# Seven products of a group in one PSUM bank, the second added by TensorE on a copy of the first

## The chip, the cores and the metric

The kernel runs on one core of a Trainium2 chip. The metric is the device time of one execution in microseconds (us), as the median of several runs. The engines of the core work side by side, each through its own list of instructions in a fixed order: TensorE (PE, matrix products into the accumulator memory PSUM), VectorE (DVE), ScalarE (ACT), GpSimd (POOL) and SyncE (SP, which starts transfers). An instruction that needs another engine's result waits on a semaphore, and everything behind it on its engine waits with it. PSUM has eight banks here, each of 128 partitions by 512 float32 columns.

## The reference

Two branches read the normalised input and are multiplied; shapes are 2048 rows by 512, the hidden layer has 1376 columns, and there are 32 heads of 16.

```python
def _A_ref(x, wqkv, wo):
    ...
    phi = lambda t: jnp.where(t > 0, t + 1, jnp.exp(t)) + 1e-6
    pq, pk = phi(q), phi(k)
    kv = jnp.einsum("bhsd,bhse->bhde", pk, v)
    z = jnp.einsum("bhsd->bhd", pk)
    num = jnp.einsum("bhqd,bhde->bhqe", pq, kv)
    den = jnp.einsum("bhqd,bhd->bhq", pq, z)[..., None] + 1e-6
    ...
    return o @ wo

def _B_ref(x, w1, w2, w3, w4):
    h = _gelu(_layernorm(x, axis=-1) @ w1)
    ...
    hs = jnp.concatenate([g0, g1, g2, g3], axis=-1) @ w2
    x1 = x + hs
    h2 = _gelu(_layernorm(x1, axis=-1) @ w3) @ w4
    return x1 + h2

xn = _layernorm(x, axis=-1)
return x + _A_ref(xn, wqkv, wo) * _silu(_B_ref(xn, w1, w2, w3, w4))
```

g0 to g3 are quarters of the columns of h, shifted by +1, -1, +2 and -2 rows.

## The kernel before, in words

The 2048 rows are worked in four quarters of 512. Every product of float32 matrices is split: each operand is a high part plus a low part (names that end in h and l), and `products` (L514) issues three matmuls for each term: high by high, high by low, low by high. All of them stand under L151 in the profile, copies and activations of ACT under L173, sums of two operands on DVE under L198.

Many of the larger products are formed by blocks in seven products instead of eight. `seven` (L948) does this for results 256 columns wide (TH = 256); it is called for 36 groups: 8 by `mix2` (L1047, the product with w2), 12 by `up_plain` and 8 by `up_pair` (L1270 and L1293, the product with w3 and its GELU), 8 by `attend_pair` (L1463). `keys_queries` (L914) does the same 512 wide, six times. Each product of a group has two terms, so six matmuls. A group takes three PSUM banks of the pool `mm`, of which `seven` uses half each: pa, pb and pe. Its steps are: product a11 b11 into pb; ACT copies pb to p1 in SBUF; product a12 b21 into pa; DVE adds pa and p1 to the first result, z[0]; s1 t1 into pe; ACT copies pe to p5; s2 t2 is accumulated on pb, and ACT copies that to u2; s4 b22 is accumulated on pe, and DVE adds u2 and pe; s3 t3 on pb, and DVE adds pb and p5; a22 t4 on pb, which is the last result. In the profile the names have m, s or k behind them for `mix2`, `attend_pair` and `keys_queries`, and none for the products with w3, where the first result is called gf.

The order of the instructions is worked out ahead by a planner (class `Plan`, L89). `add` (L99) records each operation with what it reads and writes as spans of columns of a tile; an operation depends on an earlier one where their spans of one tile overlap. With `behind` (L146) a matmul can be recorded as writing more than it does, a whole tile for example. `emit` (L296) then lists the operations by their costs and due times, engine by engine, and the code is issued in that order. A table of numbers, `SOONER` (L1746, some 170 pairs), moves the due times of single operations. The planner also hands out PSUM banks: four in the pool `acc`, four in `mm` (L475).

The semaphores are set when the planned order is issued: for each tile, an instruction that touches it waits for those issued before it on other engines that touch the same tile, if one of the two writes.

Of the kernel before, what the change touches and what calls it, by code (L numbers as in the profile page):

```python
# [9 lines left out]
F32 = mybir.dt.float32  # L10
# [5 lines left out]
P = 128  # L16
# [414 lines left out]
def linear_attn_gated_by_mixer(  # L431
# [40 lines left out]
    RB = 32  # L472

    space = bass.MemoryType.PSUM
    counts = {"w": 2, "p": 98, "h": 6, "sm": 10, "acc": 4, "mm": 4}  # L475
    const = ctx.enter_context(tc.tile_pool(name="const", bufs=1))
    pools = {}
    for tag, n in counts.items():
        kw = {"space": space} if tag in ("acc", "mm") else {}
        pools[tag] = ctx.enter_context(tc.tile_pool(name=tag, bufs=1, **kw))  # L480
    pools["dram"] = ctx.enter_context(tc.tile_pool(name="dram", bufs=1, space=bass.MemoryType.DRAM))
    pl = Plan(nc, pools, counts, ("acc", "mm"))

    def piece(name, dt=F32):
        return pl.new("p", name, dt, PIECE)[:, :512]
# [8 lines left out]
    def bank(name):  # L494
        return pl.new("mm", name, F32, 512)[:, :]
# [18 lines left out]
    def products(ps, terms, start=True, stop=True, more=False, behind=None):  # L514

        ms = []
        for sh, sl, mh, ml in terms:
            ms += [(sh, mh), (sh, ml), (sl, mh)]
        for n, (s, m) in enumerate(ms):
            pl.mm(ps, s, m, start and n == 0, stop and n == len(ms) - 1, more=more, behind=None if n else behind)  # L520
# [374 lines left out]
                TW[f"t{n + 1}"].append(hl)  # L895
        TW["b11"], TW["b21"], TW["b22"] = WK.hl[:2], WK.hl[2:], WQ.hl[2:]

    def seven_in_two(go, pb, pe, p5, first, z1, z2):

        go(pb, "a11", "b11", True)  # L900
        go(pe, "s1", "t1", True)
        pl.act(p5, pe, AF.Copy)
        pl.act(pe, pb, AF.Copy)
        go(pe, "a12", "b21", False)
        go(pb, "s2", "t2", False)
        first(pe)
        pl.act(pe, pb, AF.Copy)
        go(pb, "s3", "t3", False)
        go(pe, "s4", "b22", False)
        pl.tt(z2, pb, p5, ALU.add)  # L910
        pl.tt(z1, pe, p5, ALU.add)
        go(pb, "a22", "t4", False)

    def keys_queries(b, j):  # L914

        i, k = b * QT + j, b * QT + j + 2
        pa, pb, pe = (bank(f"{n}k{i}") for n in ("pa", "pb", "pe"))
        p1, p5, u2 = (piece(f"{n}k{i}") for n in ("p1", "p5", "u2"))

        def go(ps, x, y, start=True):  # L920
            products(ps, [both(U[b][x][c], j * P, (j + 1) * P) + TW[y][c] for c in range(2)], start, more=not start)

        go(pb, "a11", "b11")
        pl.act(p1, pb, AF.Copy)
        go(pe, "s1", "t1")
        pl.act(p5, pe, AF.Copy)
        go(pb, "s2", "t2", False)
        pl.act(u2, pb, AF.Copy)
        go(pa, "a12", "b21")
        pl.tt(p1, pa, p1, ALU.add)  # L930
        go(pb, "s3", "t3", False)
        pl.tt(p5, pb, p5, ALU.add)
        go(pe, "s4", "b22", False)
        pl.tt(u2, u2, pe, ALU.add)
        feature_k(i, p1, True)
        go(pb, "a22", "t4", False)
        feature_k(k, pb, True)
        feature_q(i, u2)
        feature_q(k, p5)
# [5 lines left out]

    def seven(name, z, prod):  # L948

        pa, pb, pe = (bank(f"{n}{name}").cols(0, TH) for n in ("pa", "pb", "pe"))  # L950
        p1, p5, u2 = (pl.new("h", f"{n}{name}", F32, TH).all for n in ("p1", "p5", "u2"))

        def go(ps, x, y, start=True):
            products(ps, prod(x, y), start, more=not start)

        go(pb, "a11", "b11")
        pl.act(p1, pb, AF.Copy)
        go(pa, "a12", "b21")
        pl.tt(z[0], pa, p1, ALU.add)
        go(pe, "s1", "t1")  # L960
        pl.act(p5, pe, AF.Copy)
        go(pb, "s2", "t2", False)
        pl.act(u2, pb, AF.Copy)
        go(pe, "s4", "b22", False)
        pl.tt(z[1], u2, pe, ALU.add)
        go(pb, "s3", "t3", False)
        pl.tt(z[2], pb, p5, ALU.add)
        go(pb, "a22", "t4", False)
        return pb

    def right(views, place):
# [75 lines left out]
    def mix2(i):  # L1047

        b, j = divmod(i, QT)
        o1, o2 = piece(f"o{i}"), piece(f"o{i + 2}")  # L1050

        def prod(x, y):
            return [both(AH[b][x], c * TH + j * P, c * TH + (j + 1) * P) + BW[y][c] for c in range(2)]

        ps = seven(f"m{i}", [o1.cols(0, TH), o1.cols(TH, 512), o2.cols(TH, 512)], prod)
        pl.act(o2.cols(0, TH), ps, AF.Copy)
        for k, o in ((i, o1), (i + 2, o2)):
            pl.gather(o, X[k])
            mixed(k, o)
# [210 lines left out]
    def up_plain(b, s):  # L1270
        hi, lo = zip(*(rounds(f"f{b}_{f}") for f in (s, s + NS)))
        c1, c2 = (piece(f"gf{b}_{f}") for f in (s, s + NS))
        z = c1.cols(0, TH), c1.cols(TH, 512), c2.cols(TH, 512)
        ps = seven(f"{b}_{s}", z, lambda x, y: [AF3[s][x][c] + YT[b][y][c] for c in range(2)])
        pl.act(hi[0], c1, AF.Gelu_apprx_tanh)
        pl.act(c1, c1, AF.Gelu_apprx_tanh)
        split(lo[0], c1, hi[0])
        pl.act(hi[1].cols(TH, 512), z[2], AF.Gelu_apprx_tanh)
        pl.act(z[2], z[2], AF.Gelu_apprx_tanh)
        pl.act(hi[1].cols(0, TH), ps, AF.Gelu_apprx_tanh)  # L1280
        pl.act(c2.cols(0, TH), ps, AF.Gelu_apprx_tanh)
        split(lo[1], c2, hi[1])
        for k, f in enumerate((s, s + NS)):
            H3[b, f] = (hi[k], lo[k], P)
# [8 lines left out]
    def up_pair(b, s):  # L1293
# [6 lines left out]
        s14, s23 = piece(f"sf{b}_{s}a"), piece(f"sf{b}_{s}b")  # L1300
        n1, n4 = s14.cols(0, TH), s14.cols(TH, 512)
        n2, n3 = s23.cols(0, TH), s23.cols(TH, 512)
        ps = seven(f"{b}_{s}", z, lambda x, y: [AF3[s][x][c] + YT[b][y][c] for c in range(2)])
        f = F4[b, s] = {}

        first = len(pl.ops)

        def keep(name, v, src):
            t = piece(f"f{b}_{s}{name}", F32R)
# [2 lines left out]
            pl.act(v, src, AF.Gelu_apprx_tanh)  # L1312
            split(f[name][1], v, f[name][0])

        pl.act(z[1], z[1], AF.Gelu_apprx_tanh)
        keep("a11", z[0], z[0])
        pl.tt(n3, z[0], z[1], ALU.subtract)
        keep("a22", z[2], z[2])
        pl.tt(n1, z[1], z[2], ALU.add)
# [6 lines left out]
        hl = rounds(f"f{b}_{s}s")  # L1326
        rounded(*hl, s14)
        f["s1"], f["s4"] = both(hl, 0, TH), both(hl, TH, 512)
        for op in pl.ops[first:]:
            op.patience = HURRY  # L1330
            pl.soon(op)

    STREAM = ("a1", "a11", "b11"), ("a4", "a22", "t4"), ("a2", "a12", "b21"), ("a5", "s1", "t1"), ("a3", "s4", "b22")
    CHAIN = None, ("s2", "t2"), ("s3", "t3")
# [128 lines left out]
    def attend_pair(i):  # L1463
        b, k = divmod(i, QT)
        k //= 2
        o1, o2 = SO[b, k, 0], SO[b, k, 1] = piece(f"so{i}"), piece(f"so{i + 1}")
        z = [o1.cols(0, TH), o1.cols(TH, 512), o2.cols(TH, 512), o2.cols(0, TH)]
# [28 lines left out]

    warm = bank("warm")
    for n in range(WARM):  # L1500
        pl.mm(warm.cols(n % NC * P, (n % NC + 1) * P), ones.all, ones.all, True, True, slow=True)
# [21 lines left out]
    scale_x(0, 1)  # L1523
    scale_x(1, 1)
    scale_x(2, 2)
    ks = [bank(f"k{i}") for i in range(QT)]
    ksum = pl.new("acc", "ksum", F32, 512).all
    for i in range(2):
        raw_k(ks[i], i)
# [136 lines left out]
    for b in range(NQ):  # L1666
# [77 lines left out]
                gate(b, QT - 1, r, a, TH, xr=xr[QT - 1], whole=a > 0)  # L1744

    SOONER = (  # L1746
# [16 lines left out]
    )  # L1763
    pl.emit(first=6.0, lead={"p": 14.0, "w": 14.0}, reserve={"p": 20, "w": 1}, window=12.0,
            ahead=6.0, table=SOONER)
# [37 lines left out]
```

## Time and profile before

| | us |
|---|---|
| median of 3 runs | 502.05 (502.02 to 502.64) |
| span of the profiled execution | 501.2 |
| PE busy | 494.3 |
| DVE busy | 440.9 |
| ACT busy | 388.9 |
| POOL busy | 84.9 |

The profiled execution has a span of 501.2 us from the first to the last instruction; its own time outside the profiler isn't listed apart, and the median is 0.85 above the span. Busy times are sums over an engine's instructions. In rows that list a group of instructions the columns are: line, engine, operation, the tile written and those read, size, count, then busy us and mean ns of one, then us of idle time ahead of them on that engine and what ended most of it. In a timeline a row is start us, duration us, engine, line, operation. A row of the waits reads: who waited for whom, us in total, times, longest. A row of the windows reads: stretch, its length, then busy us and count of PE, PEld (TensorE's loading of weights), DVE, ACT, POOL, then TensorE's granted clock, the share of the transfer engines and GB/s.

### The profile page before, as it was taken

How to read it: one execution, taken by the hardware profiler on the slowest of the kernel's cores; microseconds unless marked ns; L12 is line 12 of the kernel's file. 1: busy time of each engine (PE TensorE's matmuls, PEld its weight loads, DVE VectorE, ACT ScalarE, POOL GpSimd, SP SyncE). 2: the span in 40 equal slices, each digit the busy share in tenths (PEclk: the TensorE clock that was granted, in tenths of full speed). 3: DMA queues.
4: the chain of work that ended last, by engine and by line, in shares of the span. 5: the costliest groups of instructions: out<-in, count | busy, mean ns of one | idle time of the engine just before them, and what ended most of it. 6: DMA issues, size and time to landing. Idle time of an engine off the chain costs nothing.

```text
span 501.2 us, 9464 instructions
## 1 busy us (share of the span) xinstructions
PE 494.3 (99%) x3102; PEld 442.2 (88%) x3102; DVE 440.9 (88%) x944; ACT 388.9 (78%) x859; POOL 84.9 (17%) x97
## 2 busy tenths in 40 slices
PE   8999999999999999999999999999999999999996
PEld 6777887898888888899999989999899998999986
DVE  5989999999699995999999998897799969998364
ACT  5999899867798884977777579957699878977551
POOL 1344433131221122020100002200020200201100
PEclk9999999999999999999999999999999999999999
DMA  7949985479994799979897599978699887898604
GB/s 245 365 110 239 319 261 144 106 149 269 322 260 134 191 336 233 262 198 286 266 319 243 193 312 260 269 235 245 190 252 305 225 192 239 278 314 266 154 8 120
DMA packets 86989, 116.69 MB, mean 233 GB/s; under 512 B 8864, under 2 KB 41148, under 8 KB 86940
## 3 DMA queue, kind: packets, MB, share of 16 engines
q1 hardware_dynamic: 77004, 98.00, 60.3%
q0 software_dynamic: 9936, 18.09, 20.9%
q8 instruction: 24, 0.39, 0.3%
q14 instruction: 25, 0.20, 0.2%
HBM read 73.70 MB, written 32.91 MB: 213 GB/s over the span
## 4 chain that ended last, share of the span: by engine, by line
PE 88%; DMA 8%; SPq 1%; ACT 1%; issue 0%; DVE 0%; POOL 0%; DVEq 0%
PE a L151 15%; PE pb L151 11%; PE h L151 9%; PE pbk L151 7%; PE g L151 7%; PE acc L151 6%; PE pe L151 6%; DMA w1t<-in_w 5%; PE pbm L151 5%; PE pbs L151 4%; PE uc L151 3%; PE pek L151 3%; PE pa L151 3%; PE pem L151 2%; PE pes L151 2%; PE pak L151 2%
## 5 line engine op out<-in xcount | busy, mean ns | idle before, releaser
L230 POOL DMA_DIRECT2D th<-in_x x14 | 12.3, 926 | 164.4 <-DMA w_t<-w4t 75.6
L230 POOL DMA_DIRECT2D o<-x x16 | 14.1, 895 | 65.1 <-DVE o L198 48.0
L178 ACT ACT_TABLE_LOAD x18 | 23.1, 1283 | 0.3
L652 POOL TENSOR_TENSOR rs<-w,nhalf 128x4 f32<-128x4 f32 (+2 forms) x10 | 16.7, 1675 | 38.1 <-DVE w L203 38.1
L173 ACT ACTIVATE gf<-gf 128x256 f32<-128x256 f32 (+1 forms) x48 | 22.0, 469 | 1.2 <-DVE gf L198 0.8
L230 POOL DMA_DIRECT2D zacc<-kr x16 | 16.4, 1022 | 36.5 <-DMA zacc<-kr 13.2
L230 POOL DMA_DIRECT2D e<-x1d x12 | 10.6, 1084 | 62.0 <-DVE e L198 44.1
L208 DVE SCALAR_TENSOR_TENSOR kr<-kt,kr 128x512 f32<-128x512 f32 x16 | 11.0, 686 | 4.4 <-ACT kt L173 4.4
L173 ACT ACT_TABLE_LOAD x11 | 14.1, 1283 | 1.0 <-PEq L1794 0.8
L173 ACT ACTIVATE ht<-ht 128x512 f32<-128x512 f32 x16 | 9.8, 623 | 6.5 <-DVE ht L198 6.5
L646 DVE BATCH_NORM_STATS2 st<-o 128x6 f32<-128x512 f32 x16 | 10.6, 681 | 4.7 <-DMA o<-x 4.7
L198 DVE TENSOR_TENSOR e<-a,e 128x512 f32<-128x512 f32 (+1 forms) x17 | 9.7, 587 | 5.1 <-PE a L151 5.1
L198 DVE TENSOR_TENSOR th<-th,so 128x512 f32<-128x512 f32 (+1 forms) x17 | 10.9, 648 | 3.3 <-ACT th L173 3.3
L173 ACT ACTIVATE x<-x,nm,rs 128x512 f32<-128x512 f32 x16 | 12.9, 805 | 0.0
L173 ACT ACTIVATE p<-pe 128x256 f32<-128x256 f32 x20 | 7.6, 382 | 6.7 <-PE pe L151 6.5
L173 ACT ACTIVATE p<-pb 128x256 f32<-128x256 f32 x20 | 7.6, 381 | 6.7 <-PE pb L151 6.5
L173 ACT ACTIVATE y<-o,nm,rs 128x512 f32<-128x512 f32 x16 | 11.8, 804 | 1.2 <-DVE nm L208 1.2
L173 ACT ACTIVATE th<-e 128x512 f32<-128x512 f32 (+1 forms) x12 | 7.1, 608 | 7.1 <-DVE e L198 7.1
L208 DVE SCALAR_TENSOR_TENSOR pq<-pq,qr 128x512 f32<-128x512 f32 x12 | 8.2, 686 | 3.9 <-ACT pq L173 3.8
L198 DVE TENSOR_TENSOR ht<-h,abc 128x512 f32<-128x512 f32 x16 | 10.8, 681 | 0.4 <-PE h L151 0.4
L198 DVE TENSOR_TENSOR gf<-pb,p 128x256 f32<-128x256 f32 x20 | 8.4, 418 | 3.1 <-PE pb L151 3.0
L208 DVE SCALAR_TENSOR_TENSOR qz<-pq,zb 128x512 f32<-128x512 f32 x16 | 10.7, 684 | 0.2
(1868 smaller groups left out, 2285.1 us busy)
## 6 DMA issues: line engine op xcount, KB each, us to landing
w_s<-in_w SPq DMA_DIRECT2D x34, 256.0 KB, 4.8
w_t<-w4t SPq DMA_DIRECT2D x26, 256.0 KB, 4.5
w_b<-w4d SPq DMA_DIRECT2D x24, 256.0 KB, 5.3
x<-in_x SPq DMA_DIRECT2D x16, 256.0 KB, 6.3
zacc<-kr POOLq DMA_DIRECT2D x16, 256.0 KB, 4.8
o<-x POOLq DMA_DIRECT2D x16, 256.0 KB, 4.7
x1d<-o SPq DMA_DIRECT2D x16, 256.0 KB, 3.8
xt<-in_xt SPq DMA_DIRECT2D x15, 256.0 KB, 6.2
```

The lines of the kernel that those rows point to most:

```text
L151: lambda: nc.tensor.matmul(out.get(), lhs.get(), rhs.get(), start=start, stop=stop, skip_group_check=more))
L173: nc.scalar.activation(out.get(), src.get(), func, scale=get(scale), **kw)
L178: op.warm = lambda: nc.scalar.activation(self.scr[1].get(), self.scr[0].get(), func)
L198: self.vec(eng, out, [a, b], lambda: self.e(eng).tensor_tensor(out.get(), a.get(), b.get(), op=op), True)
L208: lambda: self.nc.vector.scalar_tensor_tensor(out.get(), a.get(), get(s), b.get(), op0=op0, op1=op1),
L230: lambda: self.nc.gpsimd.dma_start(out.get(), get(src), accum_op=ALU.add))
L646: pl.add("DVE", .62, .69, [xv], [st], lambda: nc.vector.bn_stats(st.get(), xv.get()))
L652: lambda: g.tensor_tensor(out.get(), src.get(), nh.get(), op=ALU.pow))
```

## The change

The first product of a group, a11 b11, is copied by ACT into a bank of PSUM instead of SBUF, and TensorE accumulates a12 b21 on it there; DVE's addition falls away, and ACT (a copy or GELU) reads the sum from that bank. For this there is one fixed bank, `fork`, whose two halves are taken in turn by the groups of `seven`; `keys_queries` takes all of it. pb and pe become the left and right half of one bank t (pp in the names). So a group of `seven` takes one bank of `mm` instead of three, that pool has three banks instead of four, and the pool "h" of the small copies four pieces instead of six. The GELUs of `up_plain` on the first result, 512 wide before, become two of 256. A function that nothing called is removed. The table SOONER is a new one of some 1,500 pairs, so that the whole order changes.

```diff
-    counts = {"w": 2, "p": 98, "h": 6, "sm": 10, "acc": 4, "mm": 4}
+    counts = {"w": 2, "p": 98, "h": 4, "sm": 10, "acc": 4, "mm": 3}
...
+    pools["fork"] = ctx.enter_context(tc.tile_pool(name="fork", bufs=1, space=space))
+    pl = Plan(nc, pools, counts, ("acc", "mm", "fork"))
+    fork = pl.new("fork", "fork", F32, 512)
...
     def keys_queries(b, j):
...
-        pa, pb, pe = (bank(f"{n}k{i}") for n in ("pa", "pb", "pe"))
-        p1, p5, u2 = (piece(f"{n}k{i}") for n in ("p1", "p5", "u2"))
+        pb, pe, pz = bank(f"pbk{i}"), bank(f"pek{i}"), fork.all
+        p5, u2 = (piece(f"{n}k{i}") for n in ("p5", "u2"))
...
-        pl.act(p1, pb, AF.Copy)
+        pl.act(pz, pb, AF.Copy)
...
-        go(pa, "a12", "b21")
-        pl.tt(p1, pa, p1, ALU.add)
+        go(pz, "a12", "b21", False)
+        feature_k(i, pz, True)
...
+    TURN = [0]
+
     def seven(name, z, prod):
 
-        pa, pb, pe = (bank(f"{n}{name}").cols(0, TH) for n in ("pa", "pb", "pe"))
-        p1, p5, u2 = (pl.new("h", f"{n}{name}", F32, TH).all for n in ("p1", "p5", "u2"))
-
-        def go(ps, x, y, start=True):
-            products(ps, prod(x, y), start, more=not start)
-
-        go(pb, "a11", "b11")
-        pl.act(p1, pb, AF.Copy)
-        go(pa, "a12", "b21")
-        pl.tt(z[0], pa, p1, ALU.add)
+        t = bank(f"pp{name}")
+        pb, pe = t.cols(0, TH), t.cols(TH, 512)
+        TURN[0] += 1
+        pz = fork[:, TURN[0] % 2 * TH:(TURN[0] % 2 + 1) * TH]
+        p5, u2 = (pl.new("h", f"{n}{name}", F32, TH).all for n in ("p5", "u2"))
+
+        def go(ps, x, y, start=False):
+            products(ps, prod(x, y), start, more=not start, behind=t if start else None)
+
+        go(pb, "a11", "b11", True)
+        pl.act(pz, pb, AF.Copy)
         go(pe, "s1", "t1")
         pl.act(p5, pe, AF.Copy)
-        go(pb, "s2", "t2", False)
+        go(pb, "s2", "t2")
         pl.act(u2, pb, AF.Copy)
-        go(pe, "s4", "b22", False)
+        go(pz, "a12", "b21")
+        z[0](pz)
+        go(pe, "s4", "b22")
         pl.tt(z[1], u2, pe, ALU.add)
-        go(pb, "s3", "t3", False)
+        go(pb, "s3", "t3")
         pl.tt(z[2], pb, p5, ALU.add)
-        go(pb, "a22", "t4", False)
+        go(pb, "a22", "t4")
         return pb
...
     def up_plain(b, s):
...
+        def first(ps):
+            pl.act(hi[0].cols(0, TH), ps, AF.Gelu_apprx_tanh)
+            pl.act(c1.cols(0, TH), ps, AF.Gelu_apprx_tanh)
...
-        pl.act(hi[0], c1, AF.Gelu_apprx_tanh)
-        pl.act(c1, c1, AF.Gelu_apprx_tanh)
+        pl.act(hi[0].cols(TH, 512), z[1], AF.Gelu_apprx_tanh)
+        pl.act(z[1], z[1], AF.Gelu_apprx_tanh)
...
-    ks = [bank(f"k{i}") for i in range(QT)]
+    ks = [bank(f"k{i}") for i in range(QT - 1)] + [fork.all]
...
     SOONER = (
-        2, 309, 19, 38290, 23, 20, 24, 16, 26, 2469, 31, 130, 36, 38310, 42, 1201, 43, 154, 54, 5, 55, 36, 62, 32,
...
+        0, 1178, 2, -273, 3, 225, 4, -1018, 5, -1163, 6, -54, 7, -93, 8, -1633, 9, 65, 10, 181, 11, -138, 15, 1046,
...
     )
```

In `mix2` and `attend_pair` the first entry of z becomes a copy by ACT; in `up_pair` it becomes the two GELUs that were there before, now recorded inside `seven`.

More of the change, by code (lines that the diff above doesn't have):

```diff
@@ L481, in linear_attn_gated_by_mixer @@
     pools["dram"] = ctx.enter_context(tc.tile_pool(name="dram", bufs=1, space=bass.MemoryType.DRAM))
-    pl = Plan(nc, pools, counts, ("acc", "mm"))
+    pools["fork"] = ctx.enter_context(tc.tile_pool(name="fork", bufs=1, space=space))
+    pl = Plan(nc, pools, counts, ("acc", "mm", "fork"))
+    fork = pl.new("fork", "fork", F32, 512)
     def piece(name, dt=F32):
@@ L896, in forms_kq @@
         TW["b11"], TW["b21"], TW["b22"] = WK.hl[:2], WK.hl[2:], WQ.hl[2:]
[L898 to L904, printed above, removed]
-        go(pb, "s2", "t2", False)
-        first(pe)
-        pl.act(pe, pb, AF.Copy)
-        go(pb, "s3", "t3", False)
-        go(pe, "s4", "b22", False)
-        pl.tt(z2, pb, p5, ALU.add)
-        pl.tt(z1, pe, p5, ALU.add)
-        go(pb, "a22", "t4", False)
     def keys_queries(b, j):
         i, k = b * QT + j, b * QT + j + 2
-        pa, pb, pe = (bank(f"{n}k{i}") for n in ("pa", "pb", "pe"))
-        p1, p5, u2 = (piece(f"{n}k{i}") for n in ("p1", "p5", "u2"))
+        pb, pe, pz = bank(f"pbk{i}"), bank(f"pek{i}"), fork.all
+        p5, u2 = (piece(f"{n}k{i}") for n in ("p5", "u2"))
         def go(ps, x, y, start=True):
@@ L934, in keys_queries @@
         pl.tt(u2, u2, pe, ALU.add)
-        feature_k(i, p1, True)
         go(pb, "a22", "t4", False)
@@ L944, in gram @@
             products(G[c].all, [both((xh, xl), c * P, (c + 1) * P) + (kh, kl)], i == 0, i == NT - 1)
+    TURN = [0]
     def seven(name, z, prod):
-        pa, pb, pe = (bank(f"{n}{name}").cols(0, TH) for n in ("pa", "pb", "pe"))
-        p1, p5, u2 = (pl.new("h", f"{n}{name}", F32, TH).all for n in ("p1", "p5", "u2"))
-        def go(ps, x, y, start=True):
-            products(ps, prod(x, y), start, more=not start)
-        go(pb, "a11", "b11")
-        pl.act(p1, pb, AF.Copy)
-        go(pa, "a12", "b21")
-        pl.tt(z[0], pa, p1, ALU.add)
+        t = bank(f"pp{name}")
[7 more added lines that the diff above has]
+        pl.act(pz, pb, AF.Copy)
         go(pe, "s1", "t1")
         pl.act(p5, pe, AF.Copy)
-        go(pb, "s2", "t2", False)
+        go(pb, "s2", "t2")
         pl.act(u2, pb, AF.Copy)
-        go(pe, "s4", "b22", False)
+        go(pz, "a12", "b21")
+        z[0](pz)
+        go(pe, "s4", "b22")
         pl.tt(z[1], u2, pe, ALU.add)
-        go(pb, "s3", "t3", False)
+        go(pb, "s3", "t3")
         pl.tt(z[2], pb, p5, ALU.add)
-        go(pb, "a22", "t4", False)
+        go(pb, "a22", "t4")
         return pb
@@ L1053, in prod @@
             return [both(AH[b][x], c * TH + j * P, c * TH + (j + 1) * P) + BW[y][c] for c in range(2)]
-        ps = seven(f"m{i}", [o1.cols(0, TH), o1.cols(TH, 512), o2.cols(TH, 512)], prod)
+        ps = seven(f"m{i}", [lambda v: pl.act(o1.cols(0, TH), v, AF.Copy), o1.cols(TH, 512), o2.cols(TH, 512)], prod)
         pl.act(o2.cols(0, TH), ps, AF.Copy)
@@ L1272, in up_plain @@
         c1, c2 = (piece(f"gf{b}_{f}") for f in (s, s + NS))
-        z = c1.cols(0, TH), c1.cols(TH, 512), c2.cols(TH, 512)
+        def first(ps):
+            pl.act(hi[0].cols(0, TH), ps, AF.Gelu_apprx_tanh)
+            pl.act(c1.cols(0, TH), ps, AF.Gelu_apprx_tanh)
+        z = first, c1.cols(TH, 512), c2.cols(TH, 512)
         ps = seven(f"{b}_{s}", z, lambda x, y: [AF3[s][x][c] + YT[b][y][c] for c in range(2)])
-        pl.act(hi[0], c1, AF.Gelu_apprx_tanh)
-        pl.act(c1, c1, AF.Gelu_apprx_tanh)
+        pl.act(hi[0].cols(TH, 512), z[1], AF.Gelu_apprx_tanh)
+        pl.act(z[1], z[1], AF.Gelu_apprx_tanh)
         split(lo[0], c1, hi[0])
@@ L1302, in up_pair @@
         n2, n3 = s23.cols(0, TH), s23.cols(TH, 512)
-        ps = seven(f"{b}_{s}", z, lambda x, y: [AF3[s][x][c] + YT[b][y][c] for c in range(2)])
         f = F4[b, s] = {}
-        first = len(pl.ops)
         def keep(name, v, src):
@@ L1313, in keep, with hurry, first @@
             split(f[name][1], v, f[name][0])
+        def hurry(n):
+            for op in pl.ops[n:]:
+                if op.eng != "PE":
+                    op.patience = HURRY
+                    pl.soon(op)
+        def first(ps):
+            n = len(pl.ops)
+            keep("a11", z[0], ps)
+            hurry(n)
+        ps = seven(f"{b}_{s}", (first,) + z[1:], lambda x, y: [AF3[s][x][c] + YT[b][y][c] for c in range(2)])
+        n = len(pl.ops)
         pl.act(z[1], z[1], AF.Gelu_apprx_tanh)
-        keep("a11", z[0], z[0])
         pl.tt(n3, z[0], z[1], ALU.subtract)
@@ L1328, in up_pair @@
         f["s1"], f["s4"] = both(hl, 0, TH), both(hl, TH, 512)
-        for op in pl.ops[first:]:
-            op.patience = HURRY
-            pl.soon(op)
+        hurry(n)
     STREAM = ("a1", "a11", "b11"), ("a4", "a22", "t4"), ("a2", "a12", "b21"), ("a5", "s1", "t1"), ("a3", "s4", "b22")
@@ L1466, in attend_pair @@
         o1, o2 = SO[b, k, 0], SO[b, k, 1] = piece(f"so{i}"), piece(f"so{i + 1}")
-        z = [o1.cols(0, TH), o1.cols(TH, 512), o2.cols(TH, 512), o2.cols(0, TH)]
+        z = [lambda v: pl.act(o1.cols(0, TH), v, AF.Copy), o1.cols(TH, 512), o2.cols(TH, 512), o2.cols(0, TH)]
         ps = seven(f"s{i}", z, lambda x, y: [QF[i][x][c] + M[y][c] for c in range(2)])
@@ L1495, in gate @@
         pl.store(out[rows], th)
+    fork.ap = pools["fork"].tile([P, 512], F32, name="fork")
     warm = bank("warm")
```

230 rows, old and new, of the table SOONER are left out of this document.

## The prediction, made before the result was known

> **What bounds the kernel now.** I began with the page: the busy line, the granted clock and the split of the chain that ended last.
>
> ```profile
> span 501.2 us, 9464 instructions
> PE 494.3 (99%) x3102; PEld 442.2 (88%) x3102; DVE 440.9 (88%) x944; ACT 388.9 (78%) x859; POOL 84.9 (17%) x97
> PEclk9999999999999999999999999999999999999999
> PE 88%; DMA 8%; SPq 1%; ACT 1%; issue 0%; DVE 0%; POOL 0%; DVEq 0%
> ```
>
> The tensor engine is busy for 494.3 of 501.2 us at full clock in every slice, and it is 88% of the chain. Vector engine (88%) and scalar engine (78%) are busy, but the chain hardly touches them. The next question is whether PE ever stands still in the middle, so I read its waits (these are all it has) and two stretches, engine by engine.
>
> ```profile
> PE warm L151 <- POOL ones L548: 1.7, 1, 1.7
> PE w1m L151 <- ACT w1mh L173: 0.6, 1, 0.6
> PE h L151 <- ACT w_1h L173: 0.2, 1, 0.2
> ```
>
> ```profile
> 437.50:450.00 12.50, 12.50 (x108) 12.50 (x107) 11.48 (x28) 9.18 (x22) 1.32 (x2) 1.00 1.09 311
> 450.00:462.50 12.50, 12.50 (x108) 12.50 (x107) 10.48 (x23) 9.45 (x20) 1.75 (x2) 1.00 0.87 286
> ```
>
> 2.5 us of waiting in 501: PE is full. Two things follow. Whatever the change saves on DVE or ACT buys nothing by itself. And whatever makes PE wait in the middle of a product, where nothing waits today, is paid in full, because there is no slack to pay it back from.
>
> The last row of PE before the tail, and the last row of all engines but the DMA:
>
> ```profile
> 496.67 0.28 PE L151 MATMUL a4x<-w_9h,f_9l 128*128 128x256 f32 x1
> ...
> 497.86 0.42 DVE L198 TENSOR_TENSOR th<-th,xr 128x256 f32<-128x256 f32 x1
> ```
>
> The 4.5 us from 496.67 to the end at 501.17 (one copy, two sums, the store) are the same in the new kernel.
>
> **Part 1: the adds that go.** The work removed and added, from groups by shape:
>
> ```profile
> L198 DVE TENSOR_TENSOR gf<-pa,p 128x256 f32<-128x256 f32 x20 | 8.3, 414 | 1.7 <-PE pa L151 1.7
> L198 DVE TENSOR_TENSOR p1k<-pak,p1k 128x512 f32<-128x512 f32 x6 | 4.1, 684 | 0.0
> L173 ACT ACTIVATE p<-pb 128x256 f32<-128x256 f32 x20 | 7.6, 381 | 6.7 <-PE pb L151 6.5
> L173 ACT ACTIVATE gf<-gf 128x512 f32<-128x512 f32 x12 | 7.6, 631 | 0.0
> L178 ACT ACT_TABLE_LOAD x18 | 23.1, 1283 | 0.3
> ```
>
> DVE loses 36 sums of 256 columns (the row of the largest group taken for all) and 6 of 512: 36 x 0.414 + 6 x 0.684 = 19.0 us of its 440.9. ACT, in the programs as built, gains 64 instructions of 256 columns, loses 24 of 512 and 3 table loads: 64 x 0.381 - 24 x 0.631 - 3 x 1.283 = +5.4 us on 388.9. PE's instructions are the same in number and shape. Both sums lie beside a PE that is busy 99%, so I take 0 for them; were that cover gone, ACT's share would be the 5.4 us.
>
> **Part 2: one bank where there were two.** Before, the seven products of a group accumulate in banks pa, pb and pe, each its own tile; now pb and pe are the two halves of one tile, pp, and pa's place is a half of `fork`. The planner works by columns: to it a read of the left half does not touch the right half. But the program as built makes PE and a reader of one tile take turns whichever columns they touch, and the turns go by place in the program. So I looked where readers now stand. First PE, at the first group of quarter 1 (pe, pb, pp are that group's tiles, yt11 and yt21 parts of the activations, s0 a part of w3). Before:
>
> ```order
> L151 MATMUL pe1_0_4141<-yt11h_4073,w3_0_s0h_2251 128x256 [waits Activation_49]
> L151 MATMUL pe1_0_4141<-yt11l_4081,w3_0_s0h_2251 128x256 [waits DVE_49]
> L151 MATMUL pe1_0_4141<-yt11h_4073,w3_0_s0l_2260 128x256
> L151 MATMUL pe1_0_4141<-yt11h_4073,w3_0_s0h_2251 128x256
> L151 MATMUL pb1_0_4121<-yb111h_3683,w3_0_al_2230 128x256
> L151 MATMUL pe1_0_4141<-yt11l_4081,w3_0_s0h_2251 128x256
> L151 MATMUL pe1_0_4141<-yt11h_4073,w3_0_s0l_2260 128x256
> ```
>
> And now:
>
> ```order
> L151 MATMUL pp1_0_4085<-yb111h_3316,w3_0_al_2236 128x256
> L151 MATMUL pp1_0_4085<-yt11h_3948,w3_0_s0h_1839 128x256 [waits Activation_49]
> L151 MATMUL pp1_0_4085<-yt11l_4028,w3_0_s0h_1839 128x256 [waits DVE_49]
> L151 MATMUL pp1_0_4085<-yt11h_3948,w3_0_s0l_2258 128x256
> L151 MATMUL pp1_0_4085<-yt11h_3948,w3_0_s0h_1839 128x256 [waits Activation_49]
> L151 MATMUL pp1_0_4085<-yt11l_4028,w3_0_s0h_1839 128x256
> L151 MATMUL pp1_0_4085<-yt11h_3948,w3_0_s0l_2258 128x256
> ```
>
> The second yt11h,s0h row waited for nothing; now it waits for ACT. The instruction it waits for is the copy of the left half into fork, and that copy waits for the PE row just above: with one matmul between release and wait, PE must stand still for a whole turn. The same place on ACT (p5, u2, fork: copies of the group's products; yb121, th: other work), before:
>
> ```order
> L173 ACTIVATE th3_4143<-xo3_3894 128x512 [waits DVE_49]
> L173 ACTIVATE p11_0_4153<-pb1_0_4121 128x256 [waits PE_49]
> L173 ACTIVATE p51_0_4157<-pe1_0_4141 128x256 [waits PE_49]
> L173 ACTIVATE yb121h_4162<-y1_1t_3632 128x512
> L173 ACTIVATE u21_0_4179<-pb1_0_4121 128x256 [waits PE_49]
> ```
>
> Now:
>
> ```order
> L173 ACTIVATE th2_4092<-xo2_3873 128x512 [waits DVE_49,Activation_49]
> L173 ACTIVATE fork_102<-pp1_0_4085 128x256 [waits PE_49]
> L173 ACTIVATE th3_4105<-xo3_3800 128x512 [waits DMAHW1_49,DVE_49]
> L173 ACTIVATE p51_0_4114<-pp1_0_4085 128x256 [waits PE_49]
> L173 ACTIVATE u21_0_4124<-pp1_0_4085 128x256 [waits PE_49]
> ```
>
> All three copies now read the one tile that PE writes. A second place, PE in the third group of quarter 3 (yt33, yb223, yt43: activations; s1, b: parts of w3). Before, from the last product into pe to the next into pb:
>
> ```order
> L151 MATMUL pe3_3_6799<-yb223h_6140,w3_3_s1h_3452 128x256 [waits Activation_49]
> L151 MATMUL pe3_3_6799<-yb223l_6181,w3_3_s1h_3452 128x256
> L151 MATMUL pe3_3_6799<-yb223h_6140,w3_3_s1l_3528 128x256
> L151 MATMUL pe3_3_6799<-yb223h_6140,w3_3_s1h_3452 128x256
> L151 MATMUL pe3_3_6799<-yb223l_6181,w3_3_s1h_3452 128x256
> L151 MATMUL pe3_3_6799<-yb223h_6140,w3_3_s1l_3528 128x256
> L151 MATMUL pb3_3_6761<-yt43h_6128,w3_3_b_3191 128x256 [waits DVE_49]
> ```
>
> Now (DVE reads its sums gf out of pp):
>
> ```order
> L151 MATMUL pp3_3_6640<-yt33h_5907,w3_3_s1l_3540 128x256
> L151 MATMUL pp3_3_6640<-yb223h_5897,w3_3_s1l_3540 128x256
> L151 MATMUL pp3_3_6640<-yb223h_5897,w3_3_s1h_3527 128x256
> L151 MATMUL pp3_3_6640<-yb223l_5909,w3_3_s1h_3527 128x256 [waits DVE_49]
> L151 MATMUL pp3_3_6640<-yb223h_5897,w3_3_s1l_3540 128x256
> L151 MATMUL pp3_3_6640<-yt43h_6145,w3_3_b_2988 128x256 [waits DVE_49]
> ```
>
> Before, each wait had the other bank's six matmuls in front of it. Now two turns of DVE lie within six rows, one of them inside a product.
>
> I followed every such wait in the built program. Waits of PE for a reader of the other columns of its own bank: 6 before (all in uc), 117 now. 96 of these readers wait for a PE matmul themselves. Counted in 256-wide matmuls from that matmul's start to the waiting one's (a 512-wide counts two):
> distance 1: 32 for ACT, 11 for DVE; 2: 3 and 1; 3: 8 and 2; 4: 2 and 2; 5: 5 and 4; 6: 7 for ACT; 7: 6 for ACT; beyond that, 13 in all.
>
> **The price of a turn.** The trace of before has both turns once, side by side, where PE reuses a bank with just six matmuls in between (timeline, third group of quarter 3):
>
> ```profile
> 465.12 0.28 PE L151 MATMUL pe<-yt13h,w_s0l 128*128 128x256 f32 x1
> ...
> 465.45 0.38 ACT L173 ACTIVATE p<-pe 128x256 f32<-128x256 f32 x1 [0.48 <-PE pe L151]
> ...
> 465.83 0.28 PE L151 MATMUL pb<-yt33h,w_s1l 128*128 128x256 f32 x1
> 465.88 0.19 PEld L151 LDWEIGHTS pe<-yb223h,w_s1h 128*128 128x128 f32 x1
> 465.95 0.32 PE L151 MATMUL pe<-yb223h,w_s1h 128*128 128x256 f32 x1
> ...
> 466.10 0.28 PE L151 MATMUL pe<-yb223l,w_s1h 128*128 128x256 f32 x1
> ...
> 466.20 0.42 DVE L198 TENSOR_TENSOR gf<-pb,p 128x256 f32<-128x256 f32 x1 [1.83 <-PE pb L151]
> ...
> 466.69 0.37 PE L151 MATMUL pb<-yt43h,w_b 128*128 128x256 f32 x1
> ...
> 466.90 0.28 PE L151 MATMUL pb<-yt43l,w_b 128*128 128x256 f32 x1
> ```
>
> Matmuls of 256 columns start 0.118 us apart: 465.12 to 465.83 holds six steps. ACT's turn: matmul 465.12, copy 465.45, next matmul of that bank 465.95: 0.83 from start to start; the matmul after comes 0.15 later, not 0.118, so the turn costs 0.86. DVE's: 465.83, sum 466.20, matmul 466.69: 0.86, and 0.21 to the next, so 0.95. In before both fit nearly into the six matmuls (0.71) between. A pair at distance d loses the turn less d x 0.118.
>
> ACT: 32 x 0.742 + 3 x 0.624 + 8 x 0.506 + 2 x 0.388 + 5 x 0.270 + 7 x 0.152 + 6 x 0.034 = 33.1. DVE: 11 x 0.832 + 0.714 + 2 x 0.596 + 2 x 0.478 + 4 x 0.360 = 13.5. Together 46.5 us; few pairs overlap. Readers that wait for no PE matmul add under 0.5, which I leave out.
>
> The bounds. Low: PE is off again the moment that the reader ends, and its restart costs nothing. The copy ended at 465.83, 0.71 after its matmul; the sum at 466.62, 0.79 after its. With these, the same two sums give 24.3 + 10.2 = 34.5. High: the reader stands behind other work in its queue, as here, where a 0.69 us sum of DVE sits in front:
>
> ```profile
> 215.30 0.69 DVE L198 TENSOR_TENSOR wo_2l<-wo_s,wo_2h 128x512 fp32r<-128x512 f32 x1
> 215.41 0.28 PE L151 MATMUL pbm<-w_t3h,hs33l 128*128 128x256 f32 x1
> ...
> 215.91 0.42 DVE L198 TENSOR_TENSOR o<-pbm,p5m 128x256 f32<-128x256 f32 x1
> ```
>
> The sum starts 0.50 after its matmul, not 0.37. With 0.13 more for each, 1.0 and 1.1: 41.9 + 17.4 = 59.3. I take 46.5, by the rows of the very tiles in question; queued readers are the exception there, since PE waits and its readers run dry.
>
> The Trainium skill, page "PSUM — Partial Sum Buffer", section "PSUM bank collisions raise a hardware error", says that semaphores must guard PSUM by bank, not by address, and that the hardware itself neither arbitrates nor stalls. By that rule two halves of one bank are one buffer and the sum is the 547 below; by the planner's view, columns, no turn would be due and the time would stay near 501. The built waits go by the page's rule, and before, where no bank was shared so, cannot show its price.
>
> **Part 3: the copy into fork.** It replaces a copy into SBUF of 0.381 us. Then the second product accumulates on it, so PE waits for the copy where it formerly went on into pa. The planner sees this wait (same columns), and sets the products into fork further down the order than the copy's own turn lasts. No row prices a copy into PSUM; bounded by 0 and the SBUF row, the difference is under 0.38 on a turn that PE meets later, and I take 0. The Trainium skill, page "ScalarE: Activation LUTs", section "Step-by-step: what each stage is for", holds that ScalarE reaches PSUM faster than SBUF; by it those turns would be a little shorter, and no run here shows one.
>
> **Part 4: the new order.** All instructions on POOL and SP are the same in number. The two waits of PE ahead of 45 us (0.6 and 0.2) end on a chain of gathered weights with the same work ahead of it; I count up to 1 us of small stalls as hidden in the new waits, and 2.5 us as the most.
>
> **Sum.** 501.2 + 46.5 - 1.0 = 546.7 span; the median lies 0.85 above the profiled span (502.05 - 501.2), so 547.5. Low 501.2 + 34.5 - 2.5 + 0.85 = 534.1; high 501.2 + 59.3 + 0.85 = 561.4.
>
> **The rivals.**
> *No turns (the other side).* If a waiting matmul's copy had been released long before, or PE had other rows to run first, the turn would hide. It decides at a distance of 7 to 8 matmuls (0.86/0.118 = 7.3). Then only the small stalls remain to gain: 502.05 less up to 2.5, so 499.5 to 502. For it: the planner did leave that much for same-column pairs in before, where PE waits 2.5 us in all. Against: 43 pairs stand at distance 1, and PE runs its rows in order. 0.06.
> *Half.* If only ACT's turns bite, since DVE's sums often read late: 501.2 + 33.1 + 0.85 = 535. 0.05.
> *Queued readers.* Stopped PE lets readers bunch, and each waits behind a 512-wide one (0.63 or 0.68): more than 1.1 a turn, 562 and above. For it: ACT at 78% and DVE at 88%. Against: both fall to about 72 and 77% of a 547 us span. 0.09.
> *It does not do what it says.* The sums would be gone from DVE anyway; that can be seen in the built program, so no chance of its own.
>
> **How the numbers follow.** Forecast 0.80, the three above 0.20. The range takes the bounds, rounded out to 534 and 562. A measurement can tell 0.2%, 1.0 us: the rival without turns splits evenly between faster and the same, 0.03 each; everything else is slower, 0.94.
>
> **What would show it.** In the profile after: PE's waits list "pp <- ACT fork", "pp <- ACT p", "pp <- DVE gf" with some 80 waits, a median near 0.6 us and 40 to 55 us in all; PE's busy share falls to about 91%; a turn as quoted, with matmul starts 0.8 to 0.95 apart around a copy; DVE about 422 and ACT about 394 us busy; losses spread over the groups from 50 us on, none in the last 4.5 us. Wrong, if PE waits under 10 us in all, or if matmuls of one half start 0.118 apart across a reader of the other.

## The result, and the profile after

The changed kernel takes 557.84 us (556.94 to 557.94, 4 runs) against 502.35 (502.02 to 503.11, 4 runs): a ratio of 1.110, interval 1.108 to 1.112. It is slower by 55 us, inside the stated range and 10 us above the forecast of 547.5.

The head of the page of the changed kernel:

```profile
span 556.2 us, 9511 instructions
PE 518.7 (93%) x3102; PEld 445.9 (80%) x3102; DVE 431.8 (78%) x902; ACT 392.5 (71%) x893; POOL 79.6 (14%) x97
PEclk9999999999999999999999999999999999999999
PE 75%; ACT 11%; DMA 5%; DVE 4%; issue 4%; ACTq 0%; DVEq 0%; POOLq 0%
```

PE has the same 3102 instructions at the same clock. The chain that ended last was 88% PE and is now 75%, with 11% ACT and 4% DVE in it: readers have come into the path. PE's busy time has grown by 24 us although it does the same work, and that must be read with care (below). Its waits, of which before had three lines:

```profile
PE pp L151 <- DVE gf L198: 4.9, 10, 0.6
PE pp L151 <- ACT fork L173: 4.4, 7, 1.2
PE pp L151 <- ACT p L173: 3.7, 9, 0.5
PE ppm L151 <- ACT fork L173: 3.6, 8, 0.6
PE ppm L151 <- DVE o L198: 2.5, 5, 0.6
PE pps L151 <- ACT fork L173: 2.5, 5, 0.5
PE pp L151 <- ACT u L173: 2.4, 6, 0.5
PE ppm L151 <- ACT hs13h L173: 1.4, 1, 1.4
```

These are the longest; all but one are a bank shared by a group (pp, ppm, pps) and a reader of that bank. Only hs13h is something else: an operand. Now the two places at which the prediction showed the order. The first group of quarter 1, timeline:

```profile
320.93 1.67 ACT L173 ACTIVATE th<-xo 128x512 f32<-128x512 f32 x3
...
321.23 0.28 PE L151 MATMUL pp<-yt11h,w_s0h 128*128 128x256 f32 x1
321.35 0.28 PE L151 MATMUL pp<-yt11l,w_s0h 128*128 128x256 f32 x1
321.47 0.28 PE L151 MATMUL pp<-yt11h,w_s0l 128*128 128x256 f32 x1
...
322.51 0.36 ACT L173 ACTIVATE fork<-pp 128x256 f32<-128x256 f32 x1
...
322.92 0.38 PE L151 MATMUL pp<-yt11h,w_s0h 128*128 128x256 f32 x1 [1.18 <-ACT fork L173]
323.14 0.28 PE L151 MATMUL pp<-yt11l,w_s0h 128*128 128x256 f32 x1
```

Matmuls 0.12 us apart, then one that starts 1.45 after the last, behind the copy of the other half. Here the copy itself was late: ACT had three activations of 512 columns in front of it (first row). This is the longest stall of all the pairs; the usual one looks like the second place, third group of quarter 3:

```profile
514.12 0.28 PE L151 MATMUL pp<-yb223h,w_s1h 128*128 128x256 f32 x1
...
514.51 0.42 DVE L198 TENSOR_TENSOR gf<-pp,p 128x256 f32<-128x256 f32 x1 [3.00 <-PE pp L151]
...
514.99 0.39 PE L151 MATMUL pp<-yb223l,w_s1h 128*128 128x256 f32 x1 [0.59 <-DVE gf L198]
515.21 0.28 PE L151 MATMUL pp<-yb223h,w_s1l 128*128 128x256 f32 x1
515.60 0.42 DVE L198 TENSOR_TENSOR gf<-u,pp 128x256 f32<-128x256 f32 x1 [0.67 <-PE pp L151]
...
516.08 0.39 PE L151 MATMUL pp<-yt43h,w_b 128*128 128x256 f32 x1 [0.58 <-DVE gf L198]
516.30 0.28 PE L151 MATMUL pp<-yt43l,w_b 128*128 128x256 f32 x1
```

Two turns of DVE in two us, as the order foretold. The rows also teach how much a wait in this view leaves out. From 514.12 to 514.99 PE loses 0.87 - 0.118 = 0.75 us, but the row says 0.59: idle time counts from the modelled end of the matmul before, 0.28 after its start, and that tail is counted as busy. And after the wait the next start comes 0.22 later instead of 0.118. So the bank waits add up to 28 us in the view, and PE's busy time grows, where starts tell the true loss. I therefore measured each matmul's start against the one before (0.118 us after one of 256 columns, 0.232 after one of 512) and summed what is over (steps less than 0.02 us over are left out): some 7.8 us in the kernel before, 63.7 in the changed one. The 55.9 between them is the change in span, 55.0, but for 0.6 at the start and roundings.

Of the 63.7, the 96 pairs of the prediction hold 40.3 at the waiting matmul and 8.7 at the one behind it, 49.0 in all. What is left, 14.7, is 6.9 more than before had; 3.3 of it lie at the other 21 waits for a reader of the other half, whose readers wait for no matmul.

### The profile page after: what moved, and what is told of

It is laid out like the page before. It is cut to its first block, busy times and chain, and to the rows that moved or that the text cites. A ratio compares the mean times of both kernels' runs of the same rounds, so it can differ in the third digit from the quotient of the medians.

```text
span 556.2 us, 9511 instructions
## 1 busy us (share of the span) xinstructions
PE 518.7 (93%) x3102; PEld 445.9 (80%) x3102; DVE 431.8 (78%) x902; ACT 392.5 (71%) x893; POOL 79.6 (14%) x97
## 4 chain that ended last, share of the span: by engine, by line
PE 75%; ACT 11%; DMA 5%; DVE 4%; issue 4%; ACTq 0%; DVEq 0%; POOLq 0%
PE pp L151 16%; PE a L151 13%; PE pps L151 7%; PE ppm L151 6%; PE pbk L151 5%; PE fork L151 5%; PE acc L151 5%; PE g L151 5%; PE h L151 4%; PE uc L151 3%; PE pek L151 3%; PE q L151 2%; ACT fork L173 2%; DMA o<-x 1%; DMA wq_s<-in_wqkv 1%
## 5 line engine op out<-in xcount | busy, mean ns | idle before, releaser
L654 POOL TENSOR_TENSOR rs<-w,nhalf 128x4 f32<-128x4 f32 (+2 forms) x10 | 12.0, 1203 | 50.1 <-DVE w L203 50.1
L198 DVE TENSOR_TENSOR gf<-pp,p 128x256 f32<-128x256 f32 x20 | 8.4, 420 | 12.7 <-PE pp L151 11.5
L198 DVE TENSOR_TENSOR gf<-u,pp 128x256 f32<-128x256 f32 x20 | 8.3, 417 | 12.4 <-PE pp L151 4.5
L173 ACT ACTIVATE gf<-gf 128x256 f32<-128x256 f32 x40 | 16.2, 412 | 1.7 <-DVE gf L198 1.3
L173 ACT ACTIVATE u<-pp 128x256 f32<-128x256 f32 x20 | 7.6, 382 | 8.6 <-PE pp L151 8.5
L173 ACT ACTIVATE p<-pp 128x256 f32<-128x256 f32 x20 | 7.6, 382 | 6.8 <-PE pp L151 6.7
L173 ACT ACTIVATE fork<-pp 128x256 f32<-128x256 f32 x20 | 7.4, 371 | 6.0 <-PE pp L151 5.9
```

Of the source, the lines that this page charges most:

```text
L173: nc.scalar.activation(out.get(), src.get(), func, scale=get(scale), **kw)
L198: self.vec(eng, out, [a, b], lambda: self.e(eng).tensor_tensor(out.get(), a.get(), b.get(), op=op), True)
L654: lambda: g.tensor_tensor(out.get(), src.get(), nh.get(), op=ALU.pow))
```

## The experiments

Two theories. **Turns**: the time is lost because PE and the readers of a bank take turns by bank, in an order planned by columns. **Order**: the new order itself, its queues and late operands cost it. For the parts there are two more rivals, that the copy into PSUM with the accumulation on it costs, and that a shared bank costs as such, however it is ordered.

**The turns taken out of the same order (e1).** The readers of a group's bank read a constant tile in SBUF; the planner still thinks that they read the bank, so that the order stays.

```diff
+    dummy = fixed("dummy", 256)
+    g.memset(dummy.all.get(), 1.0)
+    def apart(v):
+        return View(v.tile, v.spans, v.n, lambda ap: dummy.ap[:, 0:256])
...
-        pl.act(pz, pb, AF.Copy)
+        pl.act(pz, apart(pb), AF.Copy)
...
-        pl.tt(z[1], u2, pe, ALU.add)
+        pl.tt(z[1], u2, apart(pe), ALU.add)
```

and so for p5, u2, z[2] and the result.

> The changed kernel with its order kept, but ACT's copies, the final reads of the last product and DVE's two sums of each 256-wide group read a constant tile in SBUF instead of the group's bank (so the values of those groups are left out; the instructions, their number and order stay). PE then has nobody to take turns with in those banks. Turns theory: in the changed kernel's trace the 96 pairs of matmul and waiting matmul hold 40.3 us of stalls and 8.7 us of slow restarts; of these the program as built keeps under 1 us, so 557.8 - 49 = 509, between 503 and 513. Order theory (the new order itself, its queues and late operands cost the time): the order is the same, so 545 or more.

Measured: 509.63 us, ratio 1.016 (1.013 to 1.019). From 557.84 that is 48.2 us, where the pairs of the trace held 49.0. The page and the longest waits of this run:

```profile
PE 497.8 (98%) x3102; PEld 441.9 (87%) x3102; DVE 427.6 (84%) x902; ACT 388.8 (77%) x893; POOL 79.8 (16%) x98
```

```profile
PE ppm L151 <- ACT hs13h L173: 1.5, 1, 1.5
PE warm L151 <- POOL ones L550: 1.3, 1, 1.3
PE q L151 <- DVE kt L208: 0.5, 1, 0.5
PE fork L151 <- ACT f_4h L173: 0.5, 1, 0.5
```

With the same instructions in the same order, PE is back at 98% and every wait for a reader of the shared banks is gone. The order theory fails as the main cause; the 7.3 us over the kernel before are what it has left. The edit also takes out waits for readers of the same columns; that the loss sits at the other half is read from the 96 pairs.

The same for DVE's two sums alone (e2):

> As the one before, but only DVE's two sums of each 256-wide group read the constant tile (their values are left out); ACT still reads the bank. Turns theory: DVE's pairs held 11.3 us of stalls and 2.3 us of restarts, so 557.8 - 13.6 = 544, between 541 and 548. Order theory: 555 to 558.

Measured: 542.11 us (540.91 and 543.31), so DVE's turns were worth 15.7. The other 32.5 (542.11 - 509.63) are put down to ACT's: ACT's readers alone were not taken out in a run, but in this trace ACT's pairs hold 29.0 us at the waiting matmul, as in the changed kernel. Both sorts count.

**What the 7.3 us are (e9).** As the first run, and ACT's readers of fork (the entry z[0]) read the constant tile too.

```diff
-        z[0](pz)
+        z[0](apart(pz))
```

> As the first run (the changed kernel's order, readers of the groups' banks on a constant tile), and ACT's readers of fork in the 256-wide groups read the constant tile too (those values are left out as well). It asks what the 7.3 us are that the first run left over the kernel before. If they are waits for the reuse of fork: the 2.1 us ahead of rows into fork and 0.8 us of pairs go, 506 to 508. If they are operands that the new order brings late (4.9 us of its stalls lie between 200 and 250 us): 508 to 510.

Measured: 509.22 us (507.86 to 509.30), 0.4 below the first run and no more than its spread. The stalls ahead of rows into fork fell from 3.0 to 1.0 us, restarts counted, and most of it came back elsewhere (14.9 in all, 15.2 in the first run):

```profile
PE pps L151 <- ACT q10h L173: 1.7, 1, 1.7
PE warm L151 <- POOL ones L550: 1.3, 1, 1.3
PE ppm L151 <- ACT hs13h L173: 1.2, 1, 1.2
PE acc L151 <- ACT f_0h L173: 0.8, 1, 0.8
```

hs13h, q10h and f_0h are operands that ACT rounds for a product: they come late in this order. So the rest is the order's, as far as it could be placed; each single wait was not followed to its root.

**The shared bank alone (e3).** In the kernel before, pb and pe become halves of one bank, which the first product opens as a whole; everything else in the code stays.

```diff
-        pa, pb, pe = (bank(f"{n}{name}").cols(0, TH) for n in ("pa", "pb", "pe"))
+        pa, t = bank(f"pa{name}").cols(0, TH), bank(f"pp{name}")
+        pb, pe = t.cols(0, TH), t.cols(TH, 512)
...
-            products(ps, prod(x, y), start, more=not start)
+            products(ps, prod(x, y), start, more=not start, behind=t if ps is pb and start else None)
...
-        go(pe, "s1", "t1")
+        go(pe, "s1", "t1", False)
```

> The kernel before with one edit: pb and pe of a 256-wide group become the two halves of one bank; pa, the copy p1, DVE's sum and the table of due times stay. Turns theory: the built program has 119 waits of PE on a reader of the other half, 71 of them one matmul behind the matmul that releases the reader; by 0.75 us (ACT) and 0.86 us (DVE) less the distance, and 0.105 for each restart, 62 us, so 502 + 62 = 564, between 553 and 572. Order theory: order and table are nearly those of before, so 502 to 508.

Measured: 582.29 us, 80 more than before and above the expected range. Its waits:

```profile
PE pp L151 <- DVE gf L198: 9.8, 17, 0.9
PE pp L151 <- ACT p L173: 9.7, 18, 1.2
PE pp L151 <- ACT u L173: 6.0, 14, 0.7
...
PE a L151 <- ACT f_1a L173: 3.4, 1, 3.4
```

By starts the 119 pairs hold 55.5 and 9.7, 65.2 us against the 62 worked out from the built program. Of the other 14 us, some 3 are matmuls at half clock (granted clock 0.50 from 370.4 to 373.9 and from 513.8 to 517.2 us), the rest stalls elsewhere, such as the last row. ACT loaded its function tables 36 times, not 29; that the table of due times, fitted to other banks, is to blame is likely but not shown by this run. The turns in one bank come to more in this order than the whole loss of the change; what failed in the expectation is that the rest of the order would stay as good.

**The copy and accumulation alone (e4).** In the kernel before, three own banks to a group, the table's numbers carried over to the same operations. z[0] is ACT's copy or GELU as in the change, and `keys_queries` is edited likewise.

```diff
-        pl.act(p1, pb, AF.Copy)
-        go(pa, "a12", "b21")
-        pl.tt(z[0], pa, p1, ALU.add)
+        pl.act(pa, pb, AF.Copy)
+        go(pa, "a12", "b21", False)
+        z[0](pa)
```

> The kernel before with the copy and the accumulation alone: ACT copies the first product into bank pa, PE accumulates the second on it, ACT reads the sum from there; pa, pb and pe stay three banks, and the table of due times is that of before with its numbers carried over to the same operations. Turns theory: no wait on another half is left, 3.5 us at most of short distances on the same columns, DVE freed of 19 us that no one waits for: 501 to 506. Rival, that the copy into PSUM and the accumulation on it cost the time: 36 groups and 6 larger ones with a wait of some 0.75 us each are 30 us, so 520 to 535.

Measured: 531.00 us, ratio 1.057 (1.054 to 1.060). The number is the rival's, so I looked at where it lies:

```profile
PE a L151 <- ACT f_1a L173: 6.6, 1, 6.6
PE g L151 <- ACT k6h L173: 2.8, 1, 2.8
PE pbk L151 <- DVE p5k L198: 1.9, 1, 1.9
PE pa L151 <- ACT pa L173: 1.7, 3, 1.1
```

Waits for the copy are the last row, 1.7 us and not 30. The longest is for an operand, while ACT swaps its tables back and forth between two kinds of work:

```profile
459.47 1.28 ACT L173 ACT_TABLE_LOAD   x1
460.77 0.38 ACT L173 ACTIVATE gf<-pb 128x256 f32<-128x256 f32 x1
461.17 1.28 ACT L178 ACT_TABLE_LOAD   x1
462.46 0.20 ACT L178 ACTIVATE scr<-tiny 128x1 f32<-128x1 f32 x1
462.57 1.13 ACT L173 ACTIVATE th<-e 128x512 f32<-128x512 f32 x2
463.72 1.28 ACT L178 ACT_TABLE_LOAD   x1
```

An order whose table doesn't fit, perhaps. This was a guess until a base without any table could be set beside it. Four runs with `SOONER = ()`, the base (e5), the shared bank (e6), the copy and accumulation (e7) and the changed kernel with its planner told of whole banks (e8):

> The kernel before with an empty table of due times, as the base for the three runs beside it, so that no table fitted to one set of operations is used on another. Both theories: slower than 502 by what the fitted order was worth; from the 36 table loads and late operands of the run with the carried-over table, 510 to 535. What counts is the distance of the other three from it.

> pb and pe as halves of one bank in the kernel before, empty table. Turns theory: the built program has 62 to 64 us of turns too short, so the base of this batch plus 63, between +52 and +75. Order theory: +0 to +10, as both are unfitted.

> The copy into PSUM and TensorE's accumulation on it alone, three own banks to a group, empty table. Turns theory, with the 29 us of the run with the carried-over table put down to an order that didn't fit: within 6 us of the base, either side. Rival, that copy and accumulation cost by themselves: base plus 20 to 30.

> The changed kernel with the planner told the truth: pb, pe and the halves of fork are recorded as the whole bank, so that it plans with the turns that the program will hold; empty table. Turns theory: only 26 waits stand too close in the built program, 14 us, and 4 us on the same columns: base plus 10 to 25, and some 30 to 50 us below the changed kernel's loss in turns. Rival, that a shared bank costs as such whatever the order: base plus 45 or more.

The last one changes the planner's spans:

```diff
-        pb, pe = t.cols(0, TH), t.cols(TH, 512)
+        pb = t.tile.cut([(0, 512)], TH, lambda ap: ap[:, 0:TH])
+        pe = t.tile.cut([(0, 512)], TH, lambda ap: ap[:, TH:512])
```

| empty table | us | against the base | pairs by starts | mean granted clock | steps at half clock |
|---|---|---|---|---|---|
| kernel before (base) | 537.65 | | 0 | 0.981 | 7 |
| shared bank | 592.22 | +54.6 | 64.5 | 0.988 | 5 |
| copy and accumulation, own banks | 530.52 | -7.1 | 0 | 0.989 | 4 |
| changed kernel, planner told of whole banks | 567.55 | +29.9 | 15.7 | 0.967 | 11 |

The last column is what matmuls lost that started while the granted clock was 0.50, in us (an estimate from their starts): the unfitted orders have long waits, and TensorE loses clock behind them (last section).

The base shows that the fitted table was worth 35 us, a little more than expected. On it, the copy with the accumulation costs nothing that shows; it even gains 7 us, one more than I allowed, some 3 of them in clock. So the rival for e4's 29 us falls, and the misfit of table and order is what remains for them. One reservation: what e7 computes is some 2% off. In four of its 42 groups the accumulation goes into a bank that was last opened by a product of half the width (three in e4, none in the changed kernel with its one fixed bank); whether that is the reason is not shown. The shared bank costs 55, as expected, 10 less than its pairs hold: other stalls of the base, 43 us by starts, are 33 here. Told of whole banks, the planner takes the turns down from some 60 (worked out from the program of the changed kernel with an empty table) to 15.7. But it pays elsewhere, in clock and in long waits of PE such as 8.3 us for DVE's ht (4.3 in the base), and comes out above the expected 25. Reading and writing a bank strictly in the order of the code probably leaves it too little choice; that was not tried apart.

**A planner that knows the turns (e10 to e12).** Instead of spans, it keeps for each bank when PE's last write and the last read end, and starts nothing sooner.

```diff
+                    for u in op.tiles:
+                        if u.psum:
+                            s = max(s, u.read + self.GAP[e] if e == "PE" else u.wrote + self.GAP[e])
...
+                if e == "PE":
+                    t.wrote = op.end
+                else:
+                    t.read = op.end
```

> The changed kernel complete, with a planner that keeps, per bank, when the last matmul into it and the last reader out of it end, and starts nothing in that bank sooner, whichever columns; the table is that of the changed kernel. The built program has 1.2 us of short turns between halves and 5.7 us on the same columns. Turns theory: 49 us of stalls become 7, and the table no longer fits its order, which costs what it did in the unfitted runs, up to 35: 515 to 545, below the changed kernel. Rival, a shared bank costs as such: 550 or more.

> The same with an empty table. Short turns in the built program: 0.8 and 6.5 us. Turns theory: the unfitted base of 537.7 plus 7, so 535 to 555, and below the run told by whole banks (567.6). Rival, shared banks cost as such: 580 or more, as the kernel before with the shared bank and an empty table (592).

> The kernel before with pb and pe in one bank, an empty table and the planner that knows of turns. Short turns: 0.4 and 3.1 us. Turns theory: 537.7 plus 3, so 530 to 550, against 592.2 without that knowledge. Rival: 580 or more.

Measured: the changed kernel with its own table 530.02 us (ratio to before 1.055, 1.054 to 1.057), with an empty table 542.99; the kernel before with the shared bank and an empty table 544.45, where it was 592.22 without that knowledge. All three lie where the turns theory put them. In the first, the pairs whose reader waits for a matmul are 13, not 96, and hold 1.3 us of 34.1. Waits for other readers of the other half hold 6.6 more; among them are the longest waits, shown below the busy line:

```profile
PE 505.2 (96%) x3102; PEld 442.7 (84%) x3102; DVE 430.8 (82%) x902; ACT 397.8 (75%) x903; POOL 80.1 (15%) x97
```

```profile
PE pp L152 <- ACT fork L174: 2.4, 3, 0.8
PE pp L152 <- DVE gf L199: 2.4, 4, 0.9
PE uc L152 <- ACT e L174: 1.4, 1, 1.4
```

So a shared bank costs little as such: 6.8 us in the last run (544.45 - 537.65), against 54.6 when it is planned without its turns. None of the versions beats the kernel before, whose order had no such turn to lose.

## Why the prediction was right, and where it was off

**The bound** was right: PE had no slack, and every us that it stood still was paid.

**Turns, 46.5 forecast:** 49.0 by the trace, 48.2 by taking them out. The price was right as a whole (0.86 for ACT, measured about 0.75 + 0.105) and off in its parts, so that two errors cancelled, which is luck. ACT's turn lasts 0.74 to 0.80 from start to start in 30 of the 32 pairs at distance one, not 0.83: in the calibrating rows the restart waited a little longer. But the restart behind a wait costs 0.10 to 0.11 on ACT's turns as on DVE's, not 0.03. DVE's turn is 0.79 to 0.87. The readers that wait for no matmul, left out as under 0.5, held 3.3. And the high sum for DVE comes to 16.8 with a turn of 1.1, not 17.4, so that the high end would have been 560.8; nothing hangs on it.

**ACT's copy into fork** was taken at 0, which e7 bears out, with the reservation made there. The copy itself:

```profile
L173 ACT ACTIVATE fork<-pp 128x256 f32<-128x256 f32 x20 | 7.4, 371 | 6.0 <-PE pp L151 5.9
L173 ACT ACTIVATE p<-pp 128x256 f32<-128x256 f32 x20 | 7.6, 382 | 6.8 <-PE pp L151 6.7
```

It takes 371 ns into PSUM against 382 into SBUF from the same bank, 11 ns less. The Trainium skill, page "ScalarE: Activation LUTs", section "Step-by-step: what each stage is for", says that ScalarE reaches PSUM faster than SBUF; these rows agree.

**The step that failed is Part 4, "up to 1 us of small stalls as hidden in the new waits".** The order was worth +7.3 us, not -1: with the turns gone it still had 15.2 us of stalls, 4.9 of them between 200 and 250 us, where before had 0.6. I had read the new order only for its turns, and not for operands that arrive late; that these make up the rest was seen in the longest waits, not followed for each. The 10.3 us between forecast and result are these 8.3, 1.7 of turns (48.2 - 46.5) and 0.3 in the median of before.

**The rivals.** *No turns*: refuted by the 43 pairs at distance one, all of which stalled. *Half*: refuted by e2; DVE's turns cost 15.7. *Queued readers*: it exists, as at 322.51, but in two of the 32 pairs of ACT at distance one.

**What would show it.** PE's waits were listed as foretold, but with 28 us in bank waits, not 40 to 55, and PE busy 93%, not 91%: the view counts a matmul's tail as work. ACT's busy time went to 392.5 (394 foretold), DVE's only to 431.8 (422 foretold). Its sums went as foretold: the durations of all its rows add up to 507.5 us before and 490.1 after. But rows of DVE overlap where nothing holds them (the sums at 438.37 and 438.70 us of before start 0.33 apart and last 0.42 each), busy time counts the overlap once, and Part 1 took the full length. No one waited for it.

The Trainium skill's rule from "PSUM — Partial Sum Buffer", section "PSUM bank collisions raise a hardware error", that PSUM is to be guarded by bank and not by address, is what the program held to; e1 gives the price of the turns that it makes here. That the hardware itself does not stall could not be tried, since a wait left out would be a race.

## What to carry to other kernels

Two halves of one PSUM bank are not two buffers: where the waits go by tile, whoever writes one while others read the other takes turns with them, here 0.75 us (ACT) or 0.85 (DVE) from matmul to matmul and 0.1 for the restart, unless some seven matmuls of 256 columns (0.118 us each) stand between. A planner must know the unit that the waits go by; one rule for that recovered 28 us here. An order fitted by a table belongs to one set of operations: measure an edit against a base with the same fit, or with none, before you charge the edit with the difference.

## What was not expected of the hardware

A long standstill is paid a second time. In e4, windows around and behind PE's stall of 6.6 us (from 459.0 to 465.6) show the granted clock in the third column from the end:

```profile
450.00:456.00 6.00, 6.00 (x53) 6.00 (x52) 5.87 (x16) 5.95 (x14) 0.00 (x0) 1.00 0.85 276
460.00:463.60 3.60, 0.00 (x0) 0.00 (x0) 0.56 (x2) 3.56 (x6) 0.88 (x1) 1.00 1.07 294
463.60:467.00 3.40, 1.42 (x6) 1.43 (x7) 2.08 (x6) 3.37 (x9) 1.77 (x2) 0.50 1.11 248
467.00:470.40 3.40, 3.40 (x18) 3.40 (x17) 1.90 (x5) 2.18 (x6) 0.00 (x0) 0.50 1.08 248
470.40:474.00 3.60, 3.60 (x33) 3.60 (x32) 1.34 (x3) 1.57 (x5) 0.00 (x0) 1.00 0.51 184
```

From 463.6 to 470.4 PE has half its clock, and full clock after. Matmuls of 256 columns start about 0.21 us apart in the fourth window, not 0.118, and some 2 us are lost on top of the stall (an estimate from the starts). The stalls of the changed kernel are many but under 2 us each, and its clock stays at 1.00. The Trainium skill, "TensorE: Matmul & The Clock Gate", section "Part 1: The HAM clock gate", says that an idle window of some 3.4 us takes the clock down; these rows agree with that.
